# One PSUM tile for each bank in the dense layers, and new engine times in their planner

## The chip, the cores and the metric

The kernel runs on one core of one Trainium2 chip. The core has five engines, each with its own in-order queue of instructions: TensorE (PE, matrix products), VectorE (DVE), ScalarE (ACT), GpSimd (POOL) and SyncE (SP, which issues DMAs). They wait for one another through semaphores only. The metric is the device time of one execution in microseconds (us).

## The reference

Attention of 16 heads (2 batches of 8, 768 tokens, 64 wide), in which a query sees only the keys that fall to the same of 16 clusters, then two dense blocks over the 1536 tokens:

```python
scores = np.where(mask, scale * np.matmul(q, k.transpose(0, 1, 3, 2)), -1000000000.0)
attn = np.exp(scores - np.max(scores, axis=-1, keepdims=True))
attn = attn / (np.sum(attn, axis=-1, keepdims=True) + 1e-09)
x = np.matmul(attn, v)                       # -> 1536 tokens x 512
h = np.maximum(np.maximum(x @ w1, x @ w2), x @ w3)   # 512 -> 768
y = h @ w_out                                # 768 -> 512
r = np.maximum(y @ w_in, 0.0)                # 512 -> 2048
out = (r * r) @ w_out2                       # 2048 -> 512
```

## The kernel before

Every fp32 matrix is split into a high and a low part that PE can multiply at full rate, and a product is made of three matmuls (high by high, high by low, low by high). A matmul of the dense layers takes 128 rows of weights and 512 tokens, and its result fills one PSUM bank of 128x512 f32. PSUM has eight banks. The kernel takes them as four tiles of one bank, `pss0` to `pss3` (`ps1`), and two tiles of two banks, `psd0` and `psd1` (`ps2`, L255).

The attention comes first, until about 260 us. There a query tile's scores of 768 keys fill both banks of a `psd` tile, and DVE's maximum (L693) and ACT's exponential (L700) read both in one instruction.

The dense layers follow, and there all eight banks are single places for results: `pss_slots` (L1012) lists the two halves of each `psd` tile as two slots beside the four `pss` tiles. The first two column blocks are begun within the attention (`products`, through `psu`, L258) and finished at L1194 (`early`).

What sets the order in the dense layers is a list schedule (`arrange`, L142). Every step is entered with `op`: a due time, the engines that may do it with the time each takes, the steps that it follows, and the tiles that it opens and uses. `arrange` then walks through a model of the engines, gives each step an engine, a start and its buffers, and the instructions are issued in that order. The engine times stand at each `op` (0.69 for a DVE operation on 128x512, 0.60 for an ACT copy) or in `tt_d`, `ts_d`, `act_t` (from L1052); `LT` (L1022) is the time after which another engine sees a result; `port` says that a step of DVE or POOL takes the port that the two share. `MOE_LATER` (L85) holds one correction of the due time for each step, and the call at L1444 says from when each engine counts as free, in us from the first dense matmul.

The steps that the prediction speaks of:
- `seven` (L1126): seven products in place of eight for a pair of column blocks and two blocks of tokens, and the plain products D and E of the third block of tokens beside them. The matmuls are at L1118 (`mms`). ACT copies partial results out of PSUM (L1139) or into a bank (`seed`, L1178), DVE adds them (L1151).
- first block: the maximum over three products (DVE, L1279), and its split into high (ACT, L1285) and low (DVE, L1286), tile `h`.
- second block: ReLU and square (L1425, L1353, L1362), the split `g` (L1428, L1429), the last products (`out_mm`, six matmuls to a bank, L1373) and their sum over eight groups (`outs`: ACT's copy L1398, DVE's add L1401).
- `convert` (L1064): raw weights come by DMA (SP) and are turned and split in some ten steps of ACT, DVE and POOL (L1077 to L1096).

Of the kernel before, what the change touches and what calls it, by code (L numbers as in the profile page):

```python
# [1491 lines left out]
```

## Time and profile before

| | us |
|---|---|
| median of 3 runs (706.65, 708.63, 710.22) | 708.63 |
| the profiled execution | 709.54 |
| its span, first to last instruction | 707.8 |

| engine | busy us | share of the span | instructions |
|---|---|---|---|
| PE | 686.4 | 97% | 3573 |
| DVE | 560.7 | 79% | 903 |
| ACT | 507.0 | 72% | 977 |
| POOL | 205.6 | 29% | 235 |

The granted clock of TensorE is a share of 2.4 GHz; its mean over the span is 0.993. Times in the trace are from the start of the span. An engine's record of a matmul lasts until its result is written, longer than the step from one matmul to the next, so that records overlap and PE counts as busy in short stalls. In a row of the time line, what stands in brackets at the end is the time that the engine was idle before it, and what ended that.

### The profile page before, as it was taken

What the parts mean: (1) busy time and instruction counts of PE and PEld (TensorE: products, weight loads), DVE (VectorE), ACT (ScalarE), POOL (GpSimd) and SP (SyncE); (2) the same over time, 40 slices, a digit from 0 to 9 for tenths busy, and PEclk for the clock granted to TensorE, in tenths of its full rate; (3) what the DMA queues carried; (4) which work ended last, traced back from release to release, by engine and by line L of the source; (5) the groups of instructions that cost most, each with busy time, mean ns of one, the idle gap of its engine ahead of it and who ended that gap; (6) DMA issues with size and microseconds to landing.
All of it is one profiled execution on the core that took longest, in us unless ns stands there. A gap on an engine that the chain in (4) does not pass through costs nothing.

```text
span 707.8 us, 10259 instructions
## 1 busy us (share of the span) xinstructions
PE 686.4 (97%) x3573; PEld 582.0 (82%) x3573; DVE 560.7 (79%) x903; ACT 507.0 (72%) x977; POOL 205.6 (29%) x235
## 2 busy tenths in 40 slices
PE   7799999999999999989999999999999999999997
PEld 6689999998989877878778878888887878888886
DVE  6788989989989868789898568877867668685854
ACT  6779999999999965456464346788677776877740
POOL 6467797887858760100000000000100000000000
PEclk9899999999999999999999999999999999999999
DMA  7963726516351002212112113111311111111104
GB/s 210 249 166 109 198 71 157 134 36 162 75 149 60 2 0 98 81 34 87 59 60 89 46 45 119 60 60 60 116 55 68 59 60 61 59 63 57 60 1 178
DMA packets 21107, 62.20 MB, mean 88 GB/s; under 512 B 3168, under 2 KB 3936, under 8 KB 20608
## 3 DMA queue, kind: packets, MB, share of 16 engines
q1 hardware_dynamic: 20336, 59.98, 28.8%
q10 hardware_dynamic: 720, 1.57, 0.7%
q8 instruction: 28, 0.46, 0.3%
q14 instruction: 23, 0.19, 0.1%
HBM read 38.83 MB, written 3.15 MB: 59 GB/s over the span
## 4 chain that ended last, share of the span: by engine, by line
PE 86%; DVE 8%; ACT 3%; issue 2%; POOL 1%; DMA 0%; DVEq 0%; ACTq 0%; POOLq 0%
PE psd L1118 20%; PE pss L1118 19%; PE psd L1373 9%; PE pss L1373 8%; PE pss L723 8%; PE psd L684 5%; PE psd L686 4%; PE pss L743 4%; PE pss L744 4%; PE pss L574 2%; DVE at L734 1%; DVE nm L693 1%; ACT e L700 1%; PE pss L1194 1%; PE pss L600 1%
## 5 line engine op out<-in xcount | busy, mean ns | idle before, releaser
L734 DVE TENSOR_TENSOR at<-pss,at 128x384 fp32r<-128x384 f32 x192 | 99.8, 549 | 17.7 <-ACT at L729 17.1
L718 POOL TENSOR_SCALAR e<-e,nm 128x768 f32<-128x768 f32 x93 | 83.8, 919 | 51.2 <-DVE nm L708 30.7
L693 DVE TENSOR_REDUCE nm<-psd 128x1 f32<-128x768 f32 x96 | 90.7, 950 | 5.5 <-PE psd L686 5.1
L723 PE MATMUL pss<-ident,e 128*128 128x128 f32 x576 | 91.5, 276 | 3.0 <-DVE at L734 2.0
L729 ACT CAST at<-pss 128x384 fp32r<-128x384 f32 x192 | 85.7, 478 | 10.5 <-PE pss L723 8.7
L700 ACT ACTIVATE e<-psd,nm 128x768 f32<-128x768 f32 x96 | 87.3, 910 | 3.8 <-DVE nm L693 3.8
L723 PEld LDWEIGHTS pss<-ident,e 128*128 128x128 f32 x576 | 72.3, 141 | 12.5 <-DVE at L734 4.0
L743 PE MATMUL pss<-at,vs 128*128 128x384 f32 x192 | 73.6, 383 | 0.6 <-ACT avt L756 0.5
L1373 PE MATMUL psd<-w_wh,g_g 128*128 128x512 f32 x196 | 66.7, 390 | 0.0
L744 PE MATMUL pss<-at,vs 128*128 128x384 f32 x192 | 65.5, 341 | 0.4 <-DVE at L734 0.4
L1373 PE MATMUL pss<-w_wh,g_g 128*128 128x512 f32 (+1 forms) x192 | 63.8, 385 | 0.0
L1106 POOL TENSOR_TENSOR t_tt<-a_a 128x512 f32<-128x512 f32 x2 | 2.9, 1446 | 197.7 <-DVE a_a L1088 197.7
L1094 ACT CAST w_wh<-a_a 128x1024 fp32r<-128x1024 f32 (+1 forms) x28 | 28.6, 1022 | 25.6 <-DVE a_a L1088 25.2
L1373 PEld LDWEIGHTS psd<-w_wh,g_g 128*128 128x128 f32 x196 | 36.8, 188 | 8.3 <-ACT pss L1178 0.7
L1373 PEld LDWEIGHTS pss<-w_wh,g_g 128*128 128x128 f32 x192 | 35.9, 188 | 7.2
L1096 DVE TENSOR_TENSOR w_wl<-a_a,w_wh 128x1024 fp32r<-128x1024 f32 (+1 forms) x28 | 34.2, 1223 | 6.7 <-ACT w_wh L1094 6.5
L743 PEld LDWEIGHTS pss<-at,vs 128*128 128x128 f32 x192 | 36.5, 190 | 2.0 <-ACT avt L756 1.6
L1373 PE MATMUL psd<-w_wl,g_g 128*128 128x512 f32 x98 | 38.1, 389 | 0.0
L744 PEld LDWEIGHTS pss<-at,vs 128*128 128x128 f32 x192 | 36.7, 191 | 1.4 <-DVE at L734 1.3
L1118 PE MATMUL pss<-xT,w_wh 128*128 128x512 f32 x116 | 36.0, 392 | 1.8 <-DVE f_hm L1279 1.8
L1373 PE MATMUL pss<-w_wl,g_g 128*128 128x512 f32 (+1 forms) x96 | 36.9, 385 | 0.0
L1082 DVE SCALAR_TENSOR_TENSOR a_a<-raw_raw,a_a 128x512 uint32<-128x512 uint32 (+1 forms) x56 | 36.0, 680 | 0.7
(244 smaller groups left out, 1754.7 us busy)
## 6 DMA issues: line engine op xcount, KB each, us to landing
raw_raw<-w SPq DMA_DIRECT2D x16, 512.0 KB, 3.9
raw_raw<-win SPq DMA_DIRECT2D x16, 512.0 KB, 4.0
raw_raw<-wo SPq DMA_DIRECT2D x16, 512.0 KB, 3.6
raw_raw<-wo SPq DMA_DIRECT2D x8, 384.0 KB, 3.4
out<-acc_acc SPq DMA_DIRECT2D x11, 256.0 KB, 2.0
tv<-vv SPq DMA_DIRECT2D x7, 384.0 KB, 5.7
stodd<-rl SPq DMA_DIRECT2D x12, 192.0 KB, 4.1
stodd<-rl SPq DMA_DIRECT2D x4, 576.0 KB, 7.6
```

Of the source, the lines that this page charges most:

```text
L684: pe.matmul(pt[:, hf, :HS], t[:, 0, q], t[:, 2, hf * HS : hf * HS + HS], start=True, stop=False)
L693: dve.tensor_reduce(nms[g][:, 0, i : i + 1], pss[s][:, :, :HS], axis=AX.XY, op=ALU.max, negate=True)
L700: act.activation(two(e), pss.pop(s)[:, :, :HS], AF.Exp, bias=nm[:, 0, i : i + 1], accum_out=nm[:, 1, i : i + 1])
L718: (pool if w == "P" else dve).tensor_scalar(e, e, r, 1.0, op0=ALU.mult, op1=ALU.mult)
L723: pe.transpose(pt[:, i * P : (i + 1) * P], et[3 * g + i][:, kt * P : (kt + 1) * P], ident)
L729: act.copy(a[:, 0, :], pts[g, kt][:, :HS])
L734: eng.tensor_tensor(a[:, 1, :], pts.pop((g, kt))[:, :HS], f(a[:, 0, :]), op=ALU.subtract)
L743: pe.matmul(avs[g][:, :HS], l, a[:, 0, :], start=kt == 0, stop=False)
L744: pe.matmul(avs[g][:, :HS], l, a[:, 1, :], start=False, stop=kt == NQ - 1)
L1082: lambda e, raw=raw, c=c: e.scalar_tensor_tensor(u32(T[a][:, c]), T[raw][:, :n, 1], 0xC0000000, u32(T[a][:, c]), op0=ALU.bitwise_and, op1= ...
L1118: pe.matmul(T[bank], T[w[wi]][:, wb * P : wb * P + P], x(xi), start=first and n == 0, stop=last and n == 3 * len(ks) - 1, skip_group_check ...
L1373: pe.matmul(T[bank][:, : n.stop - n.start], T["g", 2 * g + j, c][:, a_, i * P : i * P + P], T[wt, u][:, 512 * j + n.start : 512 * j + n.stop],
```

## The change

- In the attention `psd0` and `psd1` are as before, but each has a pool of its own. When the first early product of the dense layers is issued, the pool is closed and two tiles of one bank are opened in its place (`single_banks`). The eight slots of the dense layers are then eight tiles.
- In the list schedule, a step that follows another on the same engine now starts after the end with latency on ACT, DVE and POOL too, and without it only on PE (before: on every engine but SP).
- The engine times are new: 0.602 in place of 0.69 for DVE on 128x512, 0.485 in place of 0.60 for an ACT copy from PSUM, 0.525 in place of 0.62 for an ACT cast, 1.40 and 1.42 in place of 1.47 and 1.50 for POOL, and the formulas alike; the latencies are 0.125 in place of 0.13, and 0.20 in place of 0.22 behind PE.
- All corrections of the due times (`MOE_LATER`) are new; DVE counts as free from -2.0 in place of -5.5, the shared port from -2.0 in place of 0.

```diff
@@ arrange @@
-                start[m][x] = max(start[m][x], free[e] if x == e and e != "sp" else end)
+                start[m][x] = max(start[m][x], free[e] if x == e == "pe" else end)
@@ clustered_attention_moe @@
-    ps2 = [pp.tile([P, 2, 512], F32, name=f"psd{i}") for i in range(2)]
     ps1 = [pp.tile([P, 512], F32, name=f"pss{i}") for i in range(4)]
-
-    psu = [[ps2[i][:, 0, :], ps2[i][:, 1, :], ps1[i]] for i in range(2)]
-    pso = ps1[2:]
+    pd = [ExitStack() for _ in range(2)]
+    ps2 = [pd[i].enter_context(tc.tile_pool(name=f"pd{i}", bufs=1, space=PSUM, side=SIDES[i])).tile([P, 2, 512], F32, name=f"psd{i}") for i in range(2)]
+
+    psu = [[None, None, ps1[i]] for i in range(2)]
+
+    def single_banks(i):
+
+        pd[i].close()
+        one = ctx.enter_context(tc.tile_pool(name=f"pn{i}", bufs=1, space=PSUM, side=SIDES[i]))
+        psu[i][:2] = [one.tile([P, 512], F32, name=f"psn{2 * i + j}") for j in range(2)]
...
+            def early_products(i, n, k):
+                if psu[i][0] is None:
+                    single_banks(i)
+                products(psu[i], wspl[i], k, xT, k, k == 0, k == HP - 1 and n == 0, (n,))
+
...
-    nb = len(pss_slots := [ps2[0][:, 0, :], ps2[0][:, 1, :], ps1[0], ps2[1][:, 0, :], ps2[1][:, 1, :], ps1[1], ps1[2], ps1[3]])
+    nb = len(pss_slots := [*psu[0], *psu[1], *ps1[2:]])
...
-    LT = 0.13
+    LT = 0.125
...
     def tt_d(n):
-        return 0.15 + n / 960
+        return 0.068 + n / 960
 
     def ts_d(n):
-        return 0.15 + n / 1920
+        return 0.068 + n / 1920
 
     def act_t(n):
-        return 0.22 + n / 1270
+        return 0.1 + n / 1200
...
-        op(n("R1"), key - 4, {A_: 0.6}, lambda e: seed(T[a], T[b]), [n("P1")], [("ps", a)], [b])
+        op(n("R1"), key - 4, {A_: 0.485}, lambda e: seed(T[a], T[b]), [n("P1")], [("ps", a)], [b])
...
-    order = arrange(ops, {"bank": nb, "k4": K4, "k2": K2, "raw": KR}, kinds, {"pe": 0.0, "act": -4.0, "dve": -5.5, "pool": 0.0, "sp": -16.0, "port": 0.0},
+    order = arrange(ops, {"bank": nb, "k4": K4, "k2": K2, "raw": KR}, kinds, {"pe": 0.0, "act": -4.0, "dve": -2.0, "pool": 0.0, "sp": -16.0, "port": -2.0},
```

## Rows read from the trace of the kernel before

**Rows 1.** Busy time by stretches: length, busy us (records), PEclk, DMA share, GB/s.

```profile
264.00:274.00 10.00, 8.64 (x37) 6.51 (x36) 8.92 (x12) 4.38 (x8) 1.47 (x2) 1.00 0.30 107
274.00:300.00 26.00, 26.00 (x117) 21.52 (x116) 21.11 (x31) 12.72 (x20) 2.09 (x3) 1.00 0.23 79
300.00:310.00 10.00, 8.18 (x29) 6.28 (x28) 7.21 (x10) 5.03 (x8) 2.39 (x2) 0.83 0.02 7
310.00:350.00 40.00, 40.00 (x177) 32.70 (x176) 36.16 (x52) 20.68 (x32) 0.74 (x1) 1.00 0.23 79
350.00:370.00 20.00, 19.45 (x83) 15.15 (x82) 18.49 (x28) 12.99 (x23) 0.00 (x0) 1.00 0.15 53
...
400.00:420.00 20.00, 18.30 (x80) 14.61 (x79) 10.50 (x16) 7.52 (x13) 0.00 (x0) 1.00 0.24 79
420.00:700.00 280.00, 279.24 (x1228) 229.79 (x1227) 204.52 (x289) 197.01 (x327) 3.24 (x2) 1.00 0.19 67
```

**Rows 2.** The chain that ended last: start us, us, what.

```profile
432.56 8.16 PE pss L1118 x36
```

**Rows 3.** PE's time line: start us, us, line, tiles, records, idle before.

```profile
265.53 0.73 PE L1194 MATMUL psd<-xT,whl 128*128 128x512 f32 x2 [0.20 <-POOL xT L777]
267.42 0.96 PE L1194 MATMUL psd<-xT,whl 128*128 128x512 f32 x3 [1.16 <-ACT f_hm L1206]
...
273.68 0.61 PE L1118 MATMUL pss<-xT,w_wh 128*128 128x512 f32 x2
...
295.44 0.61 PE L1118 MATMUL psd<-S_S_x,w_th 128*128 128x512 f32 x2
...
304.21 0.70 PE L1118 MATMUL pss<-xT,w_wh 128*128 128x512 f32 x2 [1.82 <-DVE f_hm L1279]
...
307.13 1.05 PE L1118 MATMUL psd<-xT,w_th 128*128 128x512 f32 x2
...
368.77 0.72 PE L1118 MATMUL psd<-xT,w_th 128*128 128x512 f32 x2 [0.28 <-DVE f_R_x L1151]
...
405.64 0.62 PE L1118 MATMUL psd<-xT,w_wh 128*128 128x512 f32 x2
...
410.69 0.50 PE L1118 MATMUL psd<-h_h,w_wh 128*128 128x512 f32 x1 [1.48 <-ACT h_h L1285]
...
533.87 0.73 PE L1118 MATMUL psd<-yT,w_wh 128*128 128x512 f32 x2 [0.68 <-ACT acc_acc L1398]
...
580.67 0.73 PE L1118 MATMUL psd<-yT,w_th 128*128 128x512 f32 x2
```

**Rows 4.** Time lines of DVE and ACT, the steps that release PE.

```profile
266.30 1.56 ACT L1206 COPY f_hm<-psd 128x512 f32<-128x512 f32 x3 [3.31 <-PE psd L1194]
...
299.72 0.69 DVE L1279 TENSOR_TENSOR f_hm<-psd,f_hm 128x512 f32<-128x512 f32 x1 [2.04 <-PE psd L1118]
...
303.39 1.27 DVE L1279 TENSOR_TENSOR f_hm<-pss,f_hm 128x512 f32<-128x512 f32 x2
...
408.56 0.69 DVE L1151 TENSOR_TENSOR f_R_x<-psd,f_R_x 128x512 f32<-128x512 f32 x1 [5.65 <-PE psd L1118]
...
533.24 0.59 ACT L1398 COPY acc_acc<-psd 128x512 f32<-128x512 f32 x1 [1.81 <-PE psd L1373]
```

**Rows 5.** Time lines of DVE and POOL where the dense layers begin.

```profile
261.90 1.29 DVE L1085 TENSOR_SCALAR a_a<-a_a 128x1024 f32<-128x1024 f32 x1 [2.92 <-ACT a_a L1077]
262.73 2.75 POOL L777 TENSOR_TENSOR xT<-xr,xT 128x384 fp32r<-128x384 f32 x2
...
264.64 1.98 DVE L1082 SCALAR_TENSOR_TENSOR a_a<-raw_raw,a_a 128x512 uint32<-128x512 uint32 x2
...
269.99 1.22 DVE L1096 TENSOR_TENSOR w_wl<-a_a,w_wh 128x1024 fp32r<-128x1024 f32 x1 [0.80 <-ACT w_wh L1094]
...
271.85 2.14 DVE L1226 TENSOR_TENSOR f_xa<-f_xa,f_xa 128x512 f32<-128x512 f32 x3
...
279.35 1.29 DVE L1082 SCALAR_TENSOR_TENSOR a_a<-raw_raw,a_a 128x512 uint32<-128x512 uint32 x2
```

More of the change, by code (lines that the diff above doesn't have):

```diff
@@ L16 @@
 PSUM = bass.MemoryType.PSUM
+SIDES = ("left", "right")
 B, H, S, D = 2, 8, 768, 64
@@ L907, in clustered_attention_moe @@
                         op(("m", i, n, k), NT + OFF["m"] + 4 * i + 2 * n + 0.5 * k,
-                           lambda i, n, k: products(psu[i], wspl[i], k, xT, k, k == 0, k == HP - 1 and n == 0, (n,)), (i, n, k), after)
+                           early_products, (i, n, k), after)
         room = {"S": 2, "T": 3, "AV": 1, "nm": 4, "e": NE, "at": 6, "avt": 2, "xr": 1, "rl": 2, "clr": 2, "tqk": 2, "tv": 1,
@@ L1027, in op @@
         assert name not in ops, name
-        e = {k: (*(v if isinstance(v, tuple) else (v, 0.22 if k == "pe" else LT)), port and k in (D_, G_)) for k, v in engines.items()}
+        e = {k: (*(v if isinstance(v, tuple) else (v, 0.2 if k == "pe" else LT)), port and k in (D_, G_)) for k, v in engines.items()}
         ops[name] = key, e, tuple(after), tuple(opens), tuple(uses)
@@ L1076, in convert @@
                lambda e, raw=raw, u=u: e.dma_start(T[raw][:, :n, :], units[u][0].bitcast(U32).rearrange("p (n t) -> p n t", t=2)), [("ld", u0)] * i, [("raw", raw)])
-            op(("ab", u), due - 9, {A_: act_t(n) + 0.05}, lambda e, raw=raw, c=c: e.activation(T[a][:, c], f(T[raw][:, :n, 1]), AF.Abs),
+            op(("ab", u), due - 9, {A_: act_t(n) + 0.03}, lambda e, raw=raw, c=c: e.activation(T[a][:, c], f(T[raw][:, :n, 1]), AF.Abs),
                [("ld", u)] + [("ab", u0)] * i, [] if i else [("a", a)], [raw, a])
-            op(("rd", u), due - 7.5, {A_: act_t(n) + 0.05}, lambda e, raw=raw, c=c: e.mul(u32(T[r][:, c]), T[raw][:, :n, 0], float(2.0**-29)),
+            op(("rd", u), due - 7.5, {A_: act_t(n) + 0.03}, lambda e, raw=raw, c=c: e.mul(u32(T[r][:, c]), T[raw][:, :n, 0], float(2.0**-29)),
                [("ld", u)] + [("rd", u0)] * i, [] if i else [("r", r)], [raw, r])
@@ L1140, in seven @@
         prod("P1", 0, b, w, [(k, X(k, 0)) for k in range(2)], xready(0, 0, 1))
-        op(n("R1"), key - 4, {A_: 0.6}, lambda e: seed(T[a], T[b]), [n("P1")], [("ps", a)], [b])
+        op(n("R1"), key - 4, {A_: 0.485}, lambda e: seed(T[a], T[b]), [n("P1")], [("ps", a)], [b])
         prod("D", 1.4, d, w, [(k, X(k, 2)) for k in range(4)], xready(2, 0, 1, 2, 3))
         prod("P6", 4.1, b, tw, [(4 + k, S(2, k)) for k in range(2)], [n("R1"), n("P1"), *sready(2)], False, False, s_(2))
-        op(n("R2"), key - 4, {A_: 0.6}, copy(2, b), [n("P6")], [("f", R(2))], [b])
+        op(n("R2"), key - 4, {A_: 0.485}, copy(2, b), [n("P6")], [("f", R(2))], [b])
         prod("P2", 5.5, a, w, [(2 + k, X(2 + k, 0)) for k in range(2)], [n("R1"), *xready(0, 2, 3)], False, False)
         prod("P7", 6.9, b, tw, [(2 + k, S(3, k)) for k in range(2)], [n("R2"), n("P6"), *sready(3)], False, False, s_(3))
-        op(n("R3"), key - 4, {A_: 0.6}, copy(3, b), [n("P7")], [("f", R(3))], [b])
+        op(n("R3"), key - 4, {A_: 0.485}, copy(3, b), [n("P7")], [("f", R(3))], [b])
         prod("P5", 8.2, c, tw, [(k, S(1, k)) for k in range(2)], sready(1), sx=s_(1))
@@ L1151, in seven @@
         add = lambda i, bank: (lambda e: e.tensor_tensor(T[R(i)], T[bank], T[R(i)], op=ALU.add))
-        op(n("C22"), key + 5, {D_: 0.69}, add(3, c), [n("P5"), n("R3")], (), [R(3), c], False)
+        op(n("C22"), key + 5, {D_: 0.602}, add(3, c), [n("P5"), n("R3")], (), [R(3), c], False)
         prod("P3", 13.6, c, w, [(6 + k, S(4, k)) for k in range(2)], [n("C22"), n("P5"), *sready(4)], False, False, s_(4))
-        op(n("C12"), key + 12, {D_: 0.69}, add(2, c), [n("P3"), n("R2")], (), [R(2), c], False)
+        op(n("C12"), key + 12, {D_: 0.602}, add(2, c), [n("P3"), n("R2")], (), [R(2), c], False)
         urgent.update(n(x) for x in ("R1", "R2", "R3", "C22"))
@@ L1205, in clustered_attention_moe @@
             hm[i, c] = ("hm", i, c)
-            op(("hc", i, c), t - 3 + c, {A_: 0.6}, lambda e, i=i, c=c: e.copy(T["hm", i, c], T["ps", "m", i, c]),
+            op(("hc", i, c), t - 3 + c, {A_: 0.485}, lambda e, i=i, c=c: e.copy(T["hm", i, c], T["ps", "m", i, c]),
                [("m", i, c)] if c else opened, [("f", hm[i, c])], [("ps", "m", i, c), hm[i, c]])
@@ L1224, in sums @@
         for j, (i, to, x, y, o) in enumerate(SUM):
-            op(("sum", tag, i, k), due + 0.8 * j, {D_: 0.69, G_: 1.5},
+            op(("sum", tag, i, k), due + 0.8 * j, {D_: 0.602, G_: 1.42},
                lambda e, to=to, x=x, y=y, o=o: e.tensor_tensor(T[tiles[to]], T[tiles[x]], T[tiles[y]], op=o), [*last[to], *last[x], *last[y]], (),
@@ L1232, in sums @@
             hi = (lambda xi, k=k: xy[:, k, xi, CH[1]]) if i == 3 else (lambda xi, s=s: T[s][:, xi, :])
-            op(("hi", *s), due + 0.8 * j + 0.5, {A_: 0.62}, lambda e, hi=hi, to=to: e.copy(hi(0), T[tiles[to]]),
+            op(("hi", *s), due + 0.8 * j + 0.5, {A_: 0.525}, lambda e, hi=hi, to=to: e.copy(hi(0), T[tiles[to]]),
                [("sum", tag, i, k)] + (after3 if i == 3 else []), [("S", s)] if i != 3 else (), [tiles[to]] + ([s] if i != 3 else []))
-            op(("lo", *s), due + 0.8 * j + 0.6, {G_: 1.47, D_: 0.69}, lambda e, hi=hi, to=to: e.tensor_tensor(hi(1), T[tiles[to]], f(hi(0)), op=ALU.subtract),
+            op(("lo", *s), due + 0.8 * j + 0.6, {G_: 1.4, D_: 0.602}, lambda e, hi=hi, to=to: e.tensor_tensor(hi(1), T[tiles[to]], f(hi(0)), op=ALU.subtract),
                [("hi", *s)], (), [tiles[to]] + ([s] if i != 3 else []))
@@ L1247, in x_sums @@
                 ready[r] = [("xa", k, r)]
-                op(("xa", k, r), t - 14 + 5 * k + 0.3 * j, {D_: 0.69, G_: 1.5},
+                op(("xa", k, r), t - 14 + 5 * k + 0.3 * j, {D_: 0.602, G_: 1.42},
                    lambda e, kk=kk, c=c, k=k, r=r: e.tensor_tensor(T["xa", k, r], f(xT[:, kk, 0, CH[c]]), f(xT[:, kk, 1, CH[c]]), op=ALU.add), (),
@@ L1275, in clustered_attention_moe @@
                 hm[fi, c] = ("hm", fi, c)
-                op(nm, at, {A_: 0.6}, lambda e, fi=fi, c=c, where=where: e.copy(T[hm[fi, c]], T[where]), [by], [("f", hm[fi, c])], [where])
+                op(nm, at, {A_: 0.485}, lambda e, fi=fi, c=c, where=where: e.copy(T[hm[fi, c]], T[where]), [by], [("f", hm[fi, c])], [where])
                 last = nm
             else:
-                op(nm, at, {D_: 0.69}, lambda e, fi=fi, c=c, where=where: e.tensor_tensor(T[hm[fi, c]], T[where], T[hm[fi, c]], op=ALU.max),
+                op(nm, at, {D_: 0.602}, lambda e, fi=fi, c=c, where=where: e.tensor_tensor(T[hm[fi, c]], T[where], T[hm[fi, c]], op=ALU.max),
                    [by, *( [("o", "x", q - 1, fo, c)] if ("o", "x", q - 1, fo, c) in ops else [("hc", fi, c)] if q == 1 else [("x", q - 1, {(1, 1): "C22", (1, 0): "C12"}[fo, c])])],
@@ L1284, in clustered_attention_moe @@
                 ht = ("h", fi, c)
-                op(("hi", *ht), at + 0.3, {A_: 0.62}, lambda e, fi=fi, c=c, ht=ht: e.copy(T[ht][:, 0, :], T[hm[fi, c]]), [last], [("h", ht)], [hm[fi, c]])
-                op(("lo", *ht), at + 0.5, {D_: 0.69, G_: 1.47}, lambda e, fi=fi, c=c, ht=ht: e.tensor_tensor(T[ht][:, 1, :], T[hm[fi, c]], f(T[ht][:, 0, :]), op=ALU.subtract),
+                op(("hi", *ht), at + 0.3, {A_: 0.525}, lambda e, fi=fi, c=c, ht=ht: e.copy(T[ht][:, 0, :], T[hm[fi, c]]), [last], [("h", ht)], [hm[fi, c]])
+                op(("lo", *ht), at + 0.5, {D_: 0.602, G_: 1.4}, lambda e, fi=fi, c=c, ht=ht: e.tensor_tensor(T[ht][:, 1, :], T[hm[fi, c]], f(T[ht][:, 0, :]), op=ALU.subtract),
                    [("hi", *ht)], (), [hm[fi, c], ht])
@@ L1321, in clustered_attention_moe @@
                 tl = ("y32", m, c)
-                op(("yc", m, c), t - 1, {A_: 0.6}, lambda e, m=m, c=c: e.copy(T["y32", m, c], T["ps", "y", m, c]), [by], [("f", tl)], [banks[c]])
+                op(("yc", m, c), t - 1, {A_: 0.485}, lambda e, m=m, c=c: e.copy(T["y32", m, c], T["ps", "y", m, c]), [by], [("f", tl)], [banks[c]])
                 yready[m, c] = [("yc", m, c)]
                 if (m < 2, c) != (True, 1):
-                    op(("hi", "y", m, c), t, {A_: 0.62}, lambda e, m=m, c=c: e.copy(y()[:, m, 0, CH[c]], T["y32", m, c]), [("yc", m, c), *lastx], (), [tl])
-                    op(("lo", "y", m, c), t + 0.5, {G_: 1.47, D_: 0.69},
+                    op(("hi", "y", m, c), t, {A_: 0.525}, lambda e, m=m, c=c: e.copy(y()[:, m, 0, CH[c]], T["y32", m, c]), [("yc", m, c), *lastx], (), [tl])
+                    op(("lo", "y", m, c), t + 0.5, {G_: 1.4, D_: 0.602},
                        lambda e, m=m, c=c: e.tensor_tensor(y()[:, m, 1, CH[c]], T["y32", m, c], f(y()[:, m, 0, CH[c]]), op=ALU.subtract), [("hi", "y", m, c)], (), [tl])
@@ L1329, in clustered_attention_moe @@
             else:
-                op(("hi", "y", m, c), t - 1, {A_: 0.6}, lambda e, m=m, c=c: e.copy(y()[:, m, 0, CH[c]], T["ps", "y", m, c]), [by, *lastx], (), [banks[c]])
-                op(("lo", "y", m, c), t - 0.8, {D_: 0.69},
+                op(("hi", "y", m, c), t - 1, {A_: 0.485}, lambda e, m=m, c=c: e.copy(y()[:, m, 0, CH[c]], T["ps", "y", m, c]), [by, *lastx], (), [banks[c]])
+                op(("lo", "y", m, c), t - 0.8, {D_: 0.602},
                    lambda e, m=m, c=c: e.tensor_tensor(y()[:, m, 1, CH[c]], T["ps", "y", m, c], f(y()[:, m, 0, CH[c]]), op=ALU.subtract), [("hi", "y", m, c)], (), [banks[c]], False)
@@ L1389, in outs @@
                 if seeded:
-                    op(("sd", g, tk), at - 1.5, {A_: 0.63}, lambda e, bank=bank, tk=tk: seed(T[bank], acc(tk)), [("oa", g - 1, tk, 0)], [("ps", bank)], [bank, to])
+                    op(("sd", g, tk), at - 1.5, {A_: 0.525}, lambda e, bank=bank, tk=tk: seed(T[bank], acc(tk)), [("oa", g - 1, tk, 0)], [("ps", bank)], [bank, to])
                 op(opn, at + 0.01 * n.start, {"pe": 6 * (w_ + 32) / 2400},
@@ L1396, in outs @@
                     new = g == 0 and tk % 2 == 0
-                    op(("oa", g, tk, n.start), at + 1, {A_: 0.6, D_: 0.69} if g == 0 else {A_: 0.6},
+                    op(("oa", g, tk, n.start), at + 1, {A_: 0.485, D_: 0.602} if g == 0 else {A_: 0.485},
                        lambda e, bank=bank, tk=tk: (e.copy if e is act else e.tensor_copy)(acc(tk), T[bank]), [opn] + ([] if new or g else [("oa", 0, tk - 1, 0)]),
@@ L1400, in outs @@
                 else:
-                    op(("oa", g, tk, n.start), at + 1, {D_: 0.15 + w_ / 960}, lambda e, bank=bank, tk=tk, n=n, w_=w_: e.tensor_tensor(acc(tk)[:, n], T[bank][:, :w_], acc(tk)[:, n], op=ALU.add),
+                    op(("oa", g, tk, n.start), at + 1, {D_: tt_d(w_)}, lambda e, bank=bank, tk=tk, n=n, w_=w_: e.tensor_tensor(acc(tk)[:, n], T[bank][:, :w_], acc(tk)[:, n], op=ALU.add),
                        [opn, ("oa", g - 1, tk, 0)], (), [bank, to], False)
@@ L1422, in clustered_attention_moe @@
             if insb:
-                op(("sq", fi, c), at, {D_: 0.7, A_: 1.26}, lambda e, v=v: positive_square(e, T[v]), [by], (), [v])
+                op(("sq", fi, c), at, {D_: 0.605, A_: 1.15}, lambda e, v=v: positive_square(e, T[v]), [by], (), [v])
             else:
-                op(("rl", fi, c), at - 1, {A_: 0.6}, lambda e, v=v, where=where: e.activation(T[v], T[where], AF.Relu), [by], [("f", v)], [where])
-                op(("sq", fi, c), at, {D_: 0.69, A_: 0.63}, lambda e, v=v: square(e, T[v]), [("rl", fi, c)], (), [v])
+                op(("rl", fi, c), at - 1, {A_: 0.485}, lambda e, v=v, where=where: e.activation(T[v], T[where], AF.Relu), [by], [("f", v)], [where])
+                op(("sq", fi, c), at, {D_: 0.602, A_: 0.53}, lambda e, v=v: square(e, T[v]), [("rl", fi, c)], (), [v])
             gt = ("g", fi, c)
-            op(("hi", *gt), at + 0.5, {A_: 0.62}, lambda e, v=v, gt=gt: e.copy(T[gt][:, 0, :], T[v]), [("sq", fi, c)], [("g", gt)], [v])
-            op(("lo", *gt), at + 1, {G_: 1.47, D_: 0.69}, lambda e, v=v, gt=gt: e.tensor_tensor(T[gt][:, 1, :], T[v], f(T[gt][:, 0, :]), op=ALU.subtract),
+            op(("hi", *gt), at + 0.5, {A_: 0.525}, lambda e, v=v, gt=gt: e.copy(T[gt][:, 0, :], T[v]), [("sq", fi, c)], [("g", gt)], [v])
+            op(("lo", *gt), at + 1, {G_: 1.4, D_: 0.602}, lambda e, v=v, gt=gt: e.tensor_tensor(T[gt][:, 1, :], T[v], f(T[gt][:, 0, :]), op=ALU.subtract),
                [("hi", *gt)], (), [v, gt])
```

104 rows, old and new, of the table MOE_LATER are left out of this document.

## The prediction

> **What bounds the kernel now.** I read the page first: TensorE (PE) is busy for 97% of the span, as in the table above. Then the busy time by stretches [rows 1]. The dense layers begin at 264.9 us and there PE is all but saturated: the chain of waits has stretches of 36 matmuls in 8.16 us, 0.2267 us each, with nothing between them [rows 2]. So the dense layers can get shorter only by the steps of PE that are longer than that, and these I count. A record lasts 0.39 us, so a stretch of L us without a stall shows (L+0.39)/0.2267 records. From 274 to 300 us that gives 116 and the row has 117: no stall. The other rows fall short: 264 to 274 shows 37 of 45.8 (2.0 us lost), 300 to 310 shows 29 of 45.8 (3.8 us), 310 to 350 177 of 178.2 (0.3), 350 to 370 83 of 89.9 (1.6), 400 to 420 80 of 89.9 (2.2), 420 to 700 1228 of 1236.8 (2.0). Together **11.9 us** of the dense part are lost; 2.0 us of them in 280 us, nearly all the rest in its first 150.
>
> Third, the instructions of PE in order of time around each loss [rows 3], and fourth those of VectorE (DVE) and ScalarE (ACT) that released it [rows 4]. What to see there: they end with a wait that the arithmetic does not need. The two-bank tiles psd0 and psd1 hold two independent results, but an engine that uses one half also waits for whoever last used the other half.
> - At 409 us DVE sits idle for 5.65 us and adds (L1151) at 408.56. The products it reads ended before 405.64, where PE goes on to twelve matmuls with xT [rows 3]: product E, in the other half. The add starts just as E ends. Through the maximum and the split of h, PE then waits until 410.69.
> - At 300 us DVE idles 2.04 us before the add at 299.72 [rows 4]. It reads the product D, which ended where the products with S begin, at 295.44 [rows 3]; what follows is again in the other half. The 2.04 us arrive at PE as the stall before 304.21, since the add that frees that bank runs at 303.39.
> - At 533 us ACT idles 1.81 us until its copy at 533.24; its own six matmuls ended one group of six earlier (1.36 us), and PE waits for the copy until 533.87.
> - At 267.42 PE itself waits for ACT, which is reading the other half since 266.30. At 368.77 PE waits for DVE's read of the other half; by the order in which the planner hands out banks its own had been free for 26 us.
>
> **The change, part by part.**
> *Four tiles of one bank.* No instruction is added or removed, PE's work is the same number of matmuls, and the attention's own tiles stay as they are; only the waits for the other half go. Each loss, with what is late next:
> 264 to 274: PE's wait before 267.42 goes. The next condition is the split of xT by GpSimd (POOL), which ended at 265.48 [rows 5], and the 265.53 row has waited for that already. Of the 2.0 us, 0.47 (that wait with its ramp) stay, so 1.5 come back.
> 300 to 310: DVE's chain starts 2.04 us earlier, so the add that ended its read for PE at 304.07 ends at 302.03; PE asks for the bank at 302.24 (304.21 less the loss of 1.98). The stall goes, with 0.2 us to spare. With it goes the slow clock behind it: the row at 307.13 has two matmuls in 1.05 us, a step of 0.43, which is the 1.2 GHz level, and the granted clock of the stretch is 0.83. Before it there is nothing but that stall. All 3.8 us come back.
> 350 to 370: 1.6 us, all of it PE waiting for the other half.
> 400 to 420: the add can start 2.7 us earlier, the loss is 2.2: all comes back.
> 420 to 700: 0.95 us at 533 comes back, for ACT could copy at 531.9; the wait of 0.31 us at 580.67 is for PE's own bank, which ACT's copy has to read, and stays; the rest are short waits for other halves. 1.7 us.
> 310 to 350: 0.3 us, I leave it.
> Sum: 1.5+3.8+1.6+2.2+1.7 = **10.8 us** of 11.9; 1.1 us stay.
>
> *New engine times and due times.* They move nothing on or off the chip; they change the order in which each engine gets its instructions, weight loads on SP's queue included. The new times are nearer the rows than the old: a copy of 128x512 from PSUM by ACT goes from 0.60 to 0.485, and three in a row take 1.56 us with the last 0.59 long, a step of 0.485 [rows 4]; two independent DVE operations of that size take 1.29 us, a step of 0.60, where the plan had 0.69 and gets 0.602; three dependent ones take 2.14, a step of 0.73, and the plan now adds its latency of 0.125 for them too [rows 5]. So what the plan holds for a stall-free order should be one more nearly. But the old times were too long by a seventh, and so left slack that the new ones don't. No row shows the new order, so I bound the stalls that it will have: not below the 1.1 us that no tile split removes, and not above those and one more stall as dear as that at 304 with its slow clock, 3.8, together 4.9. I take the middle, **3.0 us**, since the rows from 420 to 700 (0.4 us lost per 50 us) show that such a plan comes out on the chip, and those from 310 to 370, where DVE is busy for 36.2 of 40 and 18.5 of 20 us, that DVE has little to give early on.
>
> *Start values of the planner.* DVE counts as free 2.0 us before the first dense matmul instead of 5.5, and the port that DVE and POOL share likewise from -2.0 instead of 0. On the chip DVE begins at 261.90, beside POOL's split that ends at 265.48. Its four steps to 266.62 take 4.7 us; elsewhere they follow at steps of 0.6 to 0.7, some 2.7 us in all. The new plan thinks them done near 265.6 (264.9-2.0+2.7), 1 us earlier than they are; the old thought 267.7, 1 us later. The split weights end at 271.2 [rows 5], PE asks for them at 273.7 today, at 272.2 after: 1.0 us of cover is left, so I price it at nothing. If that cover is gone, it is a stall of up to 1 us, which lies within the 3.0.
> The Trainium skill (SBUF — State Buffer, section "SBUF: two separate sides") says that this shared port pair is an exclusive lock, held for the whole instruction, and that the other engine fully blocks. By that rule DVE's four steps would end 2.7 us behind POOL, at 268.2, the weights at 272.8, and PE would stall 0.6 us after the change: a forecast 0.6 us longer, 700.3. The rows have the steps slowed and yet ended at 266.6, so I go by them.
>
> **The sum.** Dense stalls go from 11.9 to 3.0 us: 8.9 us less. The profiled execution took 709.54 us (span 707.8), so it would take 700.6. The median of the runs shown is 708.63, 0.9 lower: **699.7**. The end of the kernel (last matmuls, last adds, store) is as it was.
>
> **Rivals.**
> *DVE takes the place of the wait.* With the halves apart, PE asks for the same work in less time where DVE is already busy nine tenths (310 to 370). Then only PE's direct waits for the other half come back: 1.5 + 1.6 + 0.7 (the 1.7 of 420 to 700 without the ACT copy at 533) = 3.8 us, which gives 704.8. For it: DVE's share; against: at 409 and 300 us DVE was idle, not busy, just before the stall.
> *The split does nothing.* Were the wait bound to the pair of banks and not to the tile, all would stay: 708.6. Against it: the halves become tiles of their own, and the add at 303.39, from the one-bank tile pss, is late only by DVE's own queue [rows 4].
> *Slower: the tight plan breaks.* Place: the weight conversions between 300 and 420 us. The plan without slack puts a conversion just before its use, a DVE step comes late, PE stalls two microseconds and runs at 1.2 GHz after it: 3.8 us each, as at 304. The split pays for nearly three; four of them give 708.6-10.8+15.2 = 713.0, over 0.5% slower. For it: such a stall is there already, and it drew the clock down; against: the new times fit the rows, and 1.3 us of stall at 267 drew down no clock (the next stretch has 1.00). Two or three such stalls end within 0.5%, at about 705.4 to 709.
>
> **How the numbers follow.** A measurement of this kernel can tell about 0.5% (3.5 us) from no change. Forecast (stalls of 1.1 to 4.9 us: 697.8 to 701.6, and the three runs of before lie 1.8 us to either side of their middle, so 696 to 703.4): 0.71. DVE as the bound, 704.8 or a little less: 0.12. No effect: 0.05. Two or three new stalls: 0.06. Slower: 0.06. So faster 0.83, within 0.5% 0.11, slower 0.06. The range from 696.5 to 705.0 holds the forecast and most of the first rival.
>
> **What would show it.** In the profile after: the stretch 300 to 310 with 45 matmuls and a clock of 1.00; no idle DVE of several microseconds before an L1151 add; ACT's copies and DVE's adds from PSUM starting within 0.1 us of their own six matmuls' end; PE's losses below 5 us in all. Wrong it would be if PE's steps still end on an operation of a neighbouring bank, if new idle steps of PE end on conversions (L1094, L1096) or on DMA, or if the attention, up to 255 us, takes another time than before.

## The result, and the profile after

| | before | after |
|---|---|---|
| median of 4 runs, us | 709.04 (706.65 to 710.22) | 697.92 (697.19 to 698.70) |
| the profiled execution | 709.54 | 697.19 |
| its span | 707.8 | 695.4 |
| attention: up to the first early product finished in the dense part (L1194, now L1206) | 264.94 | 263.01 |
| dense: from there to the start of the last matmul | 438.79 | 427.55 |
| end: from there to the end of the span | 4.03 | 4.83 |

The ratio is 0.9848, 95% interval 0.9819 to 0.9876: 1.5% faster, clear of the scatter, and 11.1 us in the medians, where 8.9 were forecast. The forecast was 699.7 us in a range of 696.5 to 705.0, and 697.9 lies within it. The last three lines of the table are worked out from starts in PE's time line and are used for every run below: the dense line is the one that the change was costed in. It is 11.24 us shorter. The end got 0.8 us longer, and the attention 1.9 us shorter in this profile, which is not the change's doing (below). In the rows that follow `psn` are the new tiles of one bank, and line numbers shift from kernel to kernel: the matmuls of L1118 are at L1130 after, at L1122 in e2 and at L1132 in e6 and e8.

The stretches of the profile after, in the columns of [rows 1]:

```profile
264.00:274.00 10.00, 10.00 (x46) 8.12 (x45) 9.93 (x16) 6.10 (x11) 0.00 (x0) 1.00 0.30 107
274.00:300.00 26.00, 26.00 (x116) 21.56 (x115) 24.20 (x35) 13.42 (x21) 3.09 (x3) 1.00 0.23 82
300.00:310.00 10.00, 10.00 (x45) 8.28 (x45) 9.86 (x17) 4.98 (x9) 0.00 (x0) 1.00 0.21 73
310.00:350.00 40.00, 40.00 (x178) 33.10 (x177) 37.26 (x54) 23.17 (x36) 0.74 (x1) 1.00 0.22 81
350.00:370.00 20.00, 20.00 (x90) 16.57 (x89) 14.83 (x23) 9.92 (x19) 0.74 (x1) 1.00 0.15 54
...
400.00:420.00 20.00, 20.00 (x90) 16.55 (x89) 10.55 (x15) 8.85 (x15) 0.00 (x0) 1.00 0.31 106
420.00:690.00 270.00, 270.00 (x1198) 223.75 (x1197) 194.54 (x280) 186.97 (x316) 5.95 (x5) 1.00 0.18 64
```

Each stretch holds all the matmuls that fit: 45 from 300 to 310 at a clock of 1.00, where before had 29 at 0.83, and 90 from 350 to 370 and from 400 to 420, where it had 83 and 80. The list of PE's waits from 262 us to the last matmul (who waited for whom: us in total, times, longest) has one line left, and PE's time line shows the place:

```profile
PE psn L1206 <- POOL xT L784: 0.2, 1, 0.2
```

```profile
263.01 0.39 PE L1206 MATMUL psn<-xT,whl 128*128 128x512 f32 x1
263.59 0.73 PE L1206 MATMUL psn<-xT,whl 128*128 128x512 f32 x2 [0.19 <-POOL xT L784]
264.16 3.13 PE L1206 MATMUL pss<-xT,whl 128*128 128x512 f32 x13
```

It is the wait for the split of xT, which the prediction had left standing. With its ramp it costs 0.46 us, and it is nearly all that is left: the steps of PE that are longer than 0.2267 us by 60 ns or more add up to 11.36 us in the dense part before and to 0.52 after, the other 0.06 being a wait for a split weight at 270.08 (below). So the dense part has next to nothing more to give but its matmuls; the end has.

### The profile page after: what moved, and what is told of

Its sections match the earlier page's. It is cut to its first block, busy times and chain, and to the rows that moved or that the text cites. A ratio compares the mean times of both kernels' runs of the same rounds, so it can differ in the third digit from the quotient of the medians.

```text
span 695.4 us, 10297 instructions
## 1 busy us (share of the span) xinstructions
PE 679.0 (98%) x3573; PEld 580.0 (83%) x3573; DVE 557.2 (80%) x906; ACT 502.7 (72%) x977; POOL 207.2 (30%) x238
## 4 chain that ended last, share of the span: by engine, by line
PE 89%; DVE 5%; ACT 2%; issue 1%; POOL 1%; DMA 0%; DVEq 0%; ACTq 0%; POOLq 0%
PE pss L1130 23%; PE psn L1130 18%; PE pss L1385 10%; PE psn L1385 8%; PE pss L730 7%; PE psd L691 4%; PE psd L693 4%; PE pss L750 4%; PE pss L751 4%; PE pss L581 2%; DVE at L741 2%; DVE nm L700 1%; PE pss L1206 1%; DVE acc_acc L1413 1%; PE pss L297 1%
## 5 line engine op out<-in xcount | busy, mean ns | idle before, releaser
L1385 PE MATMUL pss<-w_wh,g_g 128*128 128x512 f32 x216 | 71.4, 389 | 0.0
L1121 POOL TENSOR_TENSOR t_tt<-a_a,t_tt 128x256 f32<-128x256 f32 x3 | 2.5, 847 | 191.5 <-DVE t_tt L1118 191.5
L1385 PE MATMUL psn<-w_wh,g_g 128*128 128x512 f32 (+1 forms) x172 | 56.5, 384 | 0.0
L1385 PEld LDWEIGHTS pss<-w_wh,g_g 128*128 128x128 f32 x216 | 40.5, 188 | 8.5
L1130 PE MATMUL pss<-xT,w_wh 128*128 128x512 f32 x140 | 43.1, 389 | 0.0
L1385 PE MATMUL pss<-w_wl,g_g 128*128 128x512 f32 x108 | 42.0, 389 | 0.0
L1089 ACT ACTIVATE a_a<-raw_raw 128x512 f32<-128x512 f32 (+1 forms) x56 | 36.4, 653 | 4.1 <-DMA raw_raw<-wo 2.7
L1385 PEld LDWEIGHTS psn<-w_wh,g_g 128*128 128x128 f32 x172 | 32.1, 188 | 6.5
L1091 ACT ACTIVATE r_r<-raw_raw 128x512 uint32<-128x512 uint32 (+1 forms) x56 | 36.4, 650 | 0.7 <-PE pss L1130 0.7
```

What stands on the lines that cost most here:

```text
L1089: op(("ab", u), due - 9, {A_: act_t(n) + 0.03}, lambda e, raw=raw, c=c: e.activation(T[a][:, c], f(T[raw][:, :n, 1]), AF.Abs), [("ld", u)] ...
L1091: op(("rd", u), due - 7.5, {A_: act_t(n) + 0.03}, lambda e, raw=raw, c=c: e.mul(u32(T[r][:, c]), T[raw][:, :n, 0], float(2.0**-29)), [("ld ...
L1130: pe.matmul(T[bank], T[w[wi]][:, wb * P : wb * P + P], x(xi), start=first and n == 0, stop=last and n == 3 * len(ks) - 1, skip_group_check ...
L1385: pe.matmul(T[bank][:, : n.stop - n.start], T["g", 2 * g + j, c][:, a_, i * P : i * P + P], T[wt, u][:, 512 * j + n.start : 512 * j + n.stop],
```

## The experiments

The change has two halves, the tiles and the plan. All runs below are told by the three lines of the table; medians are beside those of the kernel before from the same chip (709.3 to 709.9).

| run | tiles split | engine times, rule, start values | due times | attention | dense | end | median (ratio, 95% interval) |
|---|---|---|---|---|---|---|---|
| before | none | old | old | 264.94 | 438.79 | 4.03 | 709.04 |
| split alone: e1 | both | old | old | 264.85 | 427.49 | 3.44 | 696.22 (0.982, 0.980 to 0.984) |
| again: e7 | both | old | old | 264.05 | 427.49 | 3.45 | 696.77 (0.982, 0.979 to 0.985) |
| again: e11 | both | old | old | 264.91 | 427.50 | 3.44 | 697.52 (0.983, 0.981 to 0.985) |
| plan alone: e2 | none | new | new | 265.61 | 435.65 | 6.16 | 707.79 (0.998, 0.997 to 1.000) |
| after again: e3 | both | new | new | 264.74 | 427.53 | 4.83 | 699.51 (0.986, 0.984 to 0.988) |
| after again: e10 | both | new | new | 265.51 | 427.59 | 4.83 | 698.96 (0.985, 0.983 to 0.987) |
| e4 | both | new | old | 264.12 | 433.28 | 3.44 | 702.45 (0.991, 0.988 to 0.993) |
| e12 | both | old | new | 265.88 | 436.10 | 4.84 | 707.76 (0.997, 0.994 to 0.999) |
| e5 | both | new | new, last groups old | 263.97 | 427.93 | 3.44 | 697.08 (0.983, 0.980 to 0.986) |
| e9 | both | new, start values old | new | 263.79 | 427.85 | 4.83 | 698.69 (0.985, 0.983 to 0.987) |
| e6 | psd1 | old | old | 266.29 | 435.32 | 4.03 | 706.48 (0.996, 0.994 to 0.997) |
| e8 | psd0 | old | old | 265.41 | 429.25 | 3.44 | 699.90 (0.986, 0.984 to 0.988) |

### Tiles or plan

e1 is the kernel before with the tiles split, its list of due times, its engine times and so the order of every engine untouched; e2 is the changed kernel with the two-bank tiles put back; e3 repeats the changed kernel beside them.

The diff is e1 against the kernel before (e7 and e11 are the same kernel); e2 has the same lines the other way round, against the changed kernel.

```diff
-    ps2 = [pp.tile([P, 2, 512], F32, name=f"psd{i}") for i in range(2)]
...
+    psu = [[None, None, ps1[i]] for i in range(2)]
...
+    def single_banks(i):
...
-    nb = len(pss_slots := [ps2[0][:, 0, :], ps2[0][:, 1, :], ps1[0], ps2[1][:, 0, :], ps2[1][:, 1, :], ps1[1], ps1[2], ps1[3]])
+    nb = len(pss_slots := [*psu[0], *psu[1], *ps1[2:]])
```

> The kernel before with nothing but the four one-bank tiles: every engine has the instructions of before in the order of before; old times, old due times. Theory (the waits for the other half are the cause): PE's losses in the dense part fall from 11.9 us to about 1.1, which gives 709.0 - 10.8 = 698.2 us (697 to 700). Rival, DVE becomes the bound: only PE's direct waits come back, 705. Rival, the order is what counts: 709, no change. The first dense matmul stands at 264.94 us in the profile of before and at 263.01 in that of after: if the new place of the tiles in PSUM shortened the attention, it is near 263 here too and near 265 in the run with the new order alone; if it is scatter between runs, it goes with neither.

> The changed kernel with the two-bank tiles kept in the dense part: the order of after on every engine, the waits for the other half back. In after's own trace, 15 steps of ACT and DVE would wait 0.1 to 2.8 us longer (most 1.37, one group of six matmuls) for the other half. Theory: some of these stall PE by 1 to 2 us each, together 4 to 7 us: 702 to 705 us. Rival, the order is what counts: 698, as the changed kernel. Rival, the order gives nothing without the split: 709 or more.

> The changed kernel itself, beside the other two on one chip: 697.9 us. Its stalls in the dense part 0.5 us as in its first profile. If the tile split is the whole gain, it lies within 1 us of the split alone; if the order gives what I left in stalls, it is 1 to 3 us faster than that.

The split alone is the whole gain, and more: 12 to 13 us in the medians, and 11.30 in the dense part (438.79 to 427.49) with not one instruction moved: in the two traces every engine has the same operations in the same order. Its list of PE's waits has the single line of the changed kernel's (L1206 on POOL, 0.2). The plan alone brings 1.5 us in the medians, barely clear of nothing (its interval ends at 0.9995). In its list every costly wait is of PE for a `psd` tile:

```profile
PE psd L1122 <- ACT psd L1182: 1.8, 3, 0.7
PE psd L1122 <- ACT f_v L1429: 1.0, 1, 1.0
PE psd L1377 <- ACT acc_acc L1402: 0.7, 1, 0.7
PE psd L1122 <- ACT f_R_y L1143: 0.7, 1, 0.7
PE psd L1377 <- ACT f_v L1429: 0.6, 1, 0.6
```

So the new order does not avoid the other half, it only meets it at other places; its dense part is 3.1 us shorter than before's and its end 2.1 longer. On top of the split the new plan costs: 3.3 us in the medians of e1 and e3, of which a repeat shows 1.4 (below).

### One tile at a time

If each stall is a wait for the other half of one certain tile, then splitting one tile must return that tile's stalls and no others. The diff is e6 against the split alone; e8 is the same with psd1 kept.

```diff
     psu = [[None, None, ps1[i]] for i in range(2)]
+    psu[0][:2] = [ps2[0][:, j, :] for j in range(2)]
+    ctx.enter_context(pd[0])
```

> The kernel before with only psd1 split into two tiles of one bank; psd0 stays a tile of two banks, the order of instructions is that of before. Theory (each stall is a wait for the other half of one particular tile): only the stalls on psd1 go, 1.44 us at 267, 0.95 at 533 and 0.31 at 650, 2.7 us together, and the stalls at 304, 351, 368 and 410 stay, with the slow clock behind the one at 304: 709.3 - 2.7 = 706.6 us. Rival (the gain of the split is something else, such as where the banks lie or how tiles are handed over between attention and dense layers, and comes with any split): 698 us or less, about all of the 12.8 us. Second rival (a stall that goes only comes back at the next wait): 709.

> The kernel before with only psd0 split; psd1 stays a tile of two banks, the order of instructions is that of before. Theory (each stall is a wait for the other half of one particular tile): the stalls on psd0 go, 3.7 us at 304 with its slow clock, 0.9 from 350 to 356, 0.55 at 368, 2.25 at 410, 0.4 at 569 and 664, 7.9 us together; those on psd1 stay (1.44 at 267, 0.95 at 533, 0.31 at 650): 709.5 - 7.9 = 701.6 us. Together with the 2.7 us of psd1 alone this makes 10.6, nearly the whole gain of splitting both. Rival (the losses of the two tiles are linked: a stall that goes on one comes back as a longer wait on the other): 704 us or more, and stalls on psd1 above 3.5 us.

With psd1 split the kernel takes 706.48, where 706.6 was expected. The stalls at 267 and 533 us are gone; those of psd0 stand. The list of PE's waits shows it, beside three waits of 0.2:

```profile
PE pss L1132 <- DVE f_hm L1293: 1.8, 1, 1.8
PE psn L1132 <- ACT h_h L1299: 1.5, 1, 1.5
```

With psd0 split one line of any size is left, ACT's copy at 533 us, now at 524, which is psd1's:

```profile
PE psd L1132 <- ACT acc_acc L1412: 0.7, 1, 0.7
```

But 699.9 is 1.7 us below the expected 701.6, for two things that I had not seen. First, the stall at 267 is gone here as well, though psd1 is still one tile. ACT's time line shows why: its first copy for the first block, 266.30 before [rows 4], runs at 263.47.

```profile
263.47 0.59 ACT L1220 COPY f_hm<-psn 128x512 f32<-128x512 f32 x1
```

Before, that copy waited for matmuls into the other half of psd0, and PE then waited for ACT on psd1: two such waits in a row, and taking away either removes the stall. (So the two single gains, 3.5 and 10.1 us from the first early product to the end, are together 1.7 more than the 11.9 of both.) Second, the end is 0.59 us shorter: before's last adds, too, waited for the other half of psd0. For the last two adds of 512 columns the wait stands in before and in e6 (2.03 us each), and it is gone there with psd0 split; before's row:

```profile
702.62 1.29 DVE L1401 TENSOR_TENSOR acc_acc<-psd,acc_acc 128x512 f32<-128x512 f32 x2 [2.03 <-PE psd L1373]
```

### What the new plan costs, and which part of it

The end is 3.44 or 3.45 us in every run of the split alone and 4.83 in every run of the changed kernel. DVE's last adds, of the changed kernel and then of e7:

```profile
684.07 0.69 DVE L1413 TENSOR_TENSOR acc_acc<-pss,acc_acc 128x512 f32<-128x512 f32 x1 [5.49 <-ACT acc_acc L1410]
685.43 0.76 DVE L1413 TENSOR_TENSOR acc_acc<-psn,acc_acc 128x256 f32<-128x256 f32 x2 [0.67 <-ACT acc_acc L1410]
686.91 2.78 DVE L1413 TENSOR_TENSOR acc_acc<-pss,acc_acc 128x512 f32<-128x512 f32 x4 [0.73 <-PE pss L1385]
689.63 2.77 DVE L1413 TENSOR_TENSOR acc_acc<-psn,acc_acc 128x512 f32<-128x512 f32 x4
```

```profile
690.43 0.69 DVE L1413 TENSOR_TENSOR acc_acc<-psn,acc_acc 128x512 f32<-128x512 f32 x1 [0.67 <-PE psn L1385]
691.15 0.42 DVE L1413 TENSOR_TENSOR acc_acc<-pss,acc_acc 128x256 f32<-128x256 f32 x1
691.86 0.42 DVE L1413 TENSOR_TENSOR acc_acc<-pss,acc_acc 128x256 f32<-128x256 f32 x1 [0.29 <-PE pss L1385]
```

In e7 DVE stands idle for 0.67 us before the last add of 512 columns and for 0.29 before the last of 256, and it is done 0.74 us after the last matmul starts (691.55). In the changed kernel DVE stands idle for 5.49 us, makes three adds with pauses of 0.7, and then eight adds in 5.49 us without a gap, of groups 6 and 7 of the same tokens in turn. The new list puts four products of group 6 last, and each of them lets two adds go, its own and that of group 7; so DVE is done 1.84 us after the last matmul starts (690.56). The span ends 2.99 us after that, with a last store of 512 columns, and in e7 2.71, with one of 256.

Which part of the plan makes it so: e4 is the changed kernel with the old due times, and e12 the split alone with the new ones.

```diff
 MOE_LATER = [
-    -51, -143, -48, -251, 72, 19, 86, -139, -238, -319, -58, -271, 40, 0, 0, 6, 88, 0, 0, 0, 88, 0, 0, 0, -151, 47, -126,
+    -370, 0, -22, -39, -172, 34, -327, 10, -233, -254, 21, -152, -67, -121, -38, 105, 216, 14, 0, -67, 216, 14, 0, -67, 0,
...
```

e5 is the changed kernel with the old due times of the last two groups alone (69 numbers), here the last line of the list:

```diff
-    68, -25, 1, 68, 0, 1, 68, -25, 1, 68, 0, 1, 68, -25, 1, 68, 0, 1, 68, -25, 1, 68, 0, 1, 68, -25, 1, 68, -25,
+    -223, -68, -142, -183, -68, -142, -223, -68, -142, -183, -68, -142, -223, -68, -142, -223,
```

And e9 has the old start values:

```diff
-    order = arrange(ops, {"bank": nb, "k4": K4, "k2": K2, "raw": KR}, kinds, {"pe": 0.0, "act": -4.0, "dve": -2.0, "pool": 0.0, "sp": -16.0, "port": -2.0},
+    order = arrange(ops, {"bank": nb, "k4": K4, "k2": K2, "raw": KR}, kinds, {"pe": 0.0, "act": -4.0, "dve": -5.5, "pool": 0.0, "sp": -16.0, "port": 0.0},
```

> The changed kernel with the old corrections of the due times put back; the split tiles, the new engine times, the rule of arrange and the start values stay. Theory (the new due times are what lengthens the end): the last products are again ordered with one 256-wide pair at the very end, so from the start of the last matmul to the end of the span it takes about 3.4 us as in the split alone, not 4.8, and the dense part has no more than about 0.5 us of stalls: 696 to 698 us. Rival (the new engine times lengthen the end, or need the new due times to be free of stalls): an end of 4.8 us, or several us of stalls in the dense part, 699 us or more.

> The changed kernel with only the due-time corrections of the last two groups of last products (groups 6 and 7, and their stores) taken from the old list, 69 numbers. Theory (what the new plan loses against the split alone sits in the last 20 us, where products of groups 6 and 7 of the same tokens come as pairs and their adds queue on VectorE): the end takes about 3.4 us in place of 4.8, and the time is 1.4 us below the changed kernel's 699.5, so about 698.1. Rival (the 3.3 us between the medians of split alone and the changed kernel lie elsewhere, in the order of the rest or in scatter): the end gets shorter or not, but the time stays within 0.5 us of 699.5.

> The kernel before with the split of both tiles and nothing else, once more, beside the others on the same chip. Theory: 696.2 us as in its first run, within 0.7, and 1.4 us or more below the changed kernel (699.5). Rival (the distance to the changed kernel was scatter between executions): 697.5 to 699.5.

> The changed kernel with the planner's start values put back (DVE free from -5.5, port from 0); everything else as changed. Theory (the prediction's: start values are worth nothing, the split weights have cover): no stall in the first 15 us of the dense layers but the wait for xT of 0.46 us, and the same time as the changed kernel within 1 us. Rival (the plan is tuned to one set of values, as e4 showed for engine times and due times): new stalls of 2 to 5 us somewhere in the dense part, since the order of some steps changes with them.

> The changed kernel once more, beside the split alone. Theory (it loses 1.4 us in the last 20 us and nothing else): 1.4 us above the split alone in the medians, and in the profiles 432.3 us from the first of the early products (L1206) to the end of the span, against 430.9. Rival (another loss, seen in the medians of the first pair as 3.3 us): 3 us or more above.

> The split of both tiles alone once more, beside the changed kernel. Theory: 696 to 697 us, 1.4 below the changed kernel. Rival: 3 us below.

> The split of both tiles with the old engine times, rule and start values, and only the new corrections of the due times: the fourth corner beside the split alone (both old), e4 (new times, old corrections) and the changed kernel (both new). Theory (the corrections are fitted to one set of engine times, and either half alone breaks the order): stalls of 2 to 10 us in the dense part, at steps whose own operation comes late, and a time of 700 us or more. Rival (the old corrections are the worse list, whatever the times): at most 0.5 us of stalls beside the wait for xT, and the changed kernel's time, 699 us.

e5 has the end of 3.44 us and 697.08, with 0.4 us more in the dense part (0.2 of it stalls at 674): the due times of the last two groups are what lengthens the end. With them put right the new plan stands level with the split alone, 0.3 us apart on the same chip.

e10 and e11, side by side: 698.96 and 697.52, 1.4 us apart, and 432.42 against 430.94 us from the first early product to the end. The three profiles of each kernel agree in that stretch within 0.07 us (432.35 to 432.42, 430.93 to 430.94). So 1.4 us is what the new plan loses. The other 1.9 of the first pair did not come back and is not in its traces either: the two profiled executions, e1's 697.58 and e3's 698.88, are 1.3 us apart, 1.4 of it behind the first early product. It lies in executions that left no trace, and its place stays open.

e4 missed its time: the end is 3.44 as the theory said, but the dense part has 5.7 us of stalls, and it takes 702.45 us, not 696 to 698. e12, the fourth corner, has 8.8 us. In e12 most is one stall with what follows it, PE's time line:

```profile
448.42 0.39 PE L1130 MATMUL pss<-S_S_y,w_tl 128*128 128x512 f32 x1
451.69 0.50 PE L1130 MATMUL pss<-S_S_y,w_th 128*128 128x512 f32 x1 [2.88 <-ACT S_S_y L1245]
...
454.17 1.05 PE L1130 MATMUL psn<-S_S_y,w_th 128*128 128x512 f32 x2
```

Here PE waits for its own operand, a sum S that ACT casts late, because DVE makes the sums before it only from 447.88 to 450.75; no tile is shared. So both lists of due times are all but free of stalls, each with its own engine times, and neither with the other's. The new engine times, nearer to the rows as they are, bring nothing by themselves (in e4 they come with the new rule and start values). e9 costs 0.3 us (0.25 of it one stall at 305 us, on a split weight): the start values move no more than that.

## Why the prediction was right

The mechanism, the place and the sign held; three terms were mis-sized, and one of them offsets part of the other two. The split gave 0.5 us more than worked out, the new order added 0.1 us of stalls where 1.9 were allowed for it (3.0 less the 1.1 that were to stay), and the end, taken as unchanged, got 0.8 us longer.

*What bounds the kernel.* 11.9 us of dense losses by counting records; 11.36 by PE's long steps, and 11.8 by e1, which gives back 11.30 and leaves 0.47. Right.

*Four tiles of one bank, 10.8 back.* Measured alone, 11.30 in the dense part (e1). The 264 to 274 and 300 to 420 us stretches came back as worked out, the slow clock behind 304 with them. Too small by 0.5, since I let the 0.31 us at 580.67 and the 0.3 from 310 to 350 stand. At 580 I saw that PE waits for ACT's copy of its own bank and stopped there; the stall stands in e6 (0.31 at 578) and is gone in e8, so the copy itself came late by a wait on psd0. The link at 267, two such waits in a row, I had read as one.

*Stalls of the new order, 3.0.* This is the step that failed most: 0.52 was measured, nearly all of it the wait for xT. The lower bound of 1.1 already held 0.6 us of other-half waits, and the upper, one more stall with a slow clock, did not come. The mechanism is real: e12 has such a stall, of 3.0 us and with a slow clock behind it. What I could not read off the trace was whether the new list fitted the new times.

*"The end is as it was."* Wrong twice: the split takes 0.59 us from it (e8), the new order adds 1.39, together the +0.80 of the table. I priced the new order only by what PE waits for. After its last matmul PE waits for nothing, and there DVE sets the time: the rival "DVE takes the place of the wait" came true in the one stretch in which I had not looked for it. That the new plan costs 1.4 us in all, near the 1.9 allowed for it, is luck: it was looked for in stalls of the dense part, and it lies at the end.

*Start values at nothing.* Right in price by e9 (0.3 us). But the cover of 1.0 us that I named was not there: it was used up. DVE's step ends at 269.98, and PE's load of these weights (PEld, its row of weight loads) waits for it:

```profile
268.76 1.22 DVE L1108 TENSOR_TENSOR w_wl<-a_a,w_wh 128x1024 fp32r<-128x1024 f32 x1
```

```profile
270.03 0.19 PEld L1130 LDWEIGHTS pss<-xT,w_wl 128*128 128x128 f32 x1 [0.21 <-DVE w_wl L1108]
```

```profile
270.08 0.45 PE L1130 MATMUL pss<-xT,w_wl 128*128 128x512 f32 x1
```

The matmul at 270.08 comes 0.06 us late, and in e3 and e10 its like comes 0.07 and 0.08 late; in the split alone it does not. Counted from the first early product, the new order has the weights ready 0.7 us later than before (6.97 against 6.27 at 271.2), as it puts five sums (L1261) between the steps of the conversion, where before had two. There is no cover left for a further shift.

On the exclusive lock of DVE's and POOL's shared port, which the Trainium skill states (SBUF — State Buffer, section "SBUF: two separate sides"), a stall of 0.6 us had been worked out for these weights; it is the 0.06 above. POOL's two steps, and DVE's two beside them with one that follows:

```profile
260.79 1.33 POOL L784 TENSOR_TENSOR xT<-xr,xT 128x384 fp32r<-128x384 f32 x1
```

```profile
262.07 1.46 POOL L784 TENSOR_TENSOR xT<-xr,xT 128x384 fp32r<-128x384 f32 x1
```

```profile
261.17 1.49 DVE L1261 TENSOR_TENSOR f_xa<-xT 128x512 f32<-128x512 f32 x1
262.59 1.50 DVE L1099 TENSOR_SCALAR a_a<-a_a 128x1024 uint32<-128x1024 uint32 x1
264.01 0.68 DVE L1261 TENSOR_TENSOR f_xa<-xT 128x512 f32<-128x512 f32 x1
```

Both engines are drawn out: DVE's sum takes 0.68 us afterwards, and POOL's operation takes 1.0 in the attention. And they end in turn: DVE's first step 0.55 us behind POOL's first (262.12), POOL's second 0.9 behind DVE's first (262.66), and DVE's second 0.55 behind POOL's second (263.54). This agrees with a lock that is held for one instruction. What was wrong was my working, which let POOL keep it through both of its steps; DVE was not held back to POOL's end.

*The sum.* 8.9 less was forecast. Dense 11.24 less and end 0.80 more make 10.44; the medians say 11.1, and the attention scatters by more than what is between. Its length in the profile after, 263.0 us against 264.9, is one of the signs that I had named for being wrong; the three profiles of the changed kernel spread as far by themselves, from 263.0 to 265.5.

*Rivals.* That the split does nothing falls with e1. DVE as the bound of the dense part falls: from 310 to 350 it is busy for 37.26 of 40 us, more than before, and PE waits for nothing. The tight plan that breaks is seen after only in the 0.06 us at 270.08, and in earnest in e4 and e12.

## What to carry to other kernels

A tile is what waits are kept by in this program: two independent results in one tile wait for each other's users, on PE, DVE and ACT alike, and the trace shows it as an idle engine whose own input ended one group earlier. Undo that first, with the order left alone; it was the whole gain here, and a plan tuned anew beside it took 1.4 us back at the very end, where the bound passes from PE to the last engine of the chain. Corrections of a plan belong to the times that they were found with: exchange both or neither.
